# Decays of two more opening units by transfers, masks and exponentials; two more units turned on VectorE; a new order of work in an mLSTM + MLP kernel

## The chip, the cores and the metric

One core of one Trainium2 chip runs the whole program. The metric is the device time of one execution in microseconds (us); the kernel before stands at the median of three runs. Engines are named as in the profile: PE (TensorE's matmuls), PEld (its weight loads), DVE (VectorE), ACT (ScalarE), POOL (GpSimd), SP (SyncE, which here only issues transfers).

## The reference

An mLSTM layer (batch 4, 8 heads, 768 steps, head size 40) and behind it a feed-forward layer, all in float32:

```python
for t in range(S):
    m_new = np.maximum(f_gate[:, :, t] + m, i_gate[:, :, t])
    f_stab = np.exp(f_gate[:, :, t] + m - m_new)
    i_stab = np.exp(i_gate[:, :, t] - m_new)
    m = m_new
    C = f_stab[..., None, None] * C + i_stab[..., None, None] * np.einsum('bhd,bhe->bhde', vt, kt)
    n = f_stab[..., None] * n + i_stab[..., None] * kt
    y[:, :, t] = sigmoid(o_gate[:, :, t]) * (C @ qt) / max(|n @ qt|, 1)
x = y as [3072 tokens, 320]
h = x @ w_in                       # 320 -> 2048
out = (h * sigmoid(h)) @ w_out     # 2048 -> 320
```

## The kernel before

**Units.** The sequence is cut into 6 chunks of 128 steps. A unit is one chunk of one batch row with all 8 heads: unit n is chunk n // 4 of row n % 4, 24 in all. Units 0 to 3 are thus the first chunk. For a unit the kernel needs the decay matrix D, exp of a difference of running gate sums with the later keys masked out, in blocks of 64 steps. There are two ways to D:

- units below `WIDE` = 4 build it in PSUM on PE: `spread` (8 matmuls), `spans` (16) and `keys` (4) add up the exponent with its mask, and one ACT instruction takes the exponential of the whole tile (`exps_all`, L585);
- the others fetch the gate sums LF, which DVE computed and SP stored to DRAM (`LFd`), spread over partitions (`load_d`, two transfers, L500), set the masked half to -1e30 on POOL (`mask`, twice, L601), and take exponentials head by head on ACT (`exps`, two halves of four instructions, L595) with the key's term as bias. That term is `aT`, which `flip` makes on PE (L267, L272) and DVE copies out.

Then follow, for every unit: `column` (DVE, L615: values weighted by the last column of D), `products` (PE, L642: the state's increment), `carry` (ACT, POOL and DVE: the state), `scores` (PE, L679: q times k), `weigh` (DVE, L698: scores times D), `values` (PE, L716), `queries` (PE, L739: q scaled on POOL by L628, times the state) and `gate` (DVE, L757 to L770: division, output gate).

**Turning.** A unit's result x has tokens on partitions, and the feed-forward product wants features there. Units below `TURN` = 8 turn it with transposes on PE into PSUM (`xpose`, L798 to L801). The others turn 32x32 blocks on DVE (`turn`, L779), write them to DRAM in four transfers, and read them back as whole rows (`turned`). In both ways ACT then rounds the high part (L808) and DVE takes the low part (L812).

**The feed-forward part.** Every product is made of rounded high and low parts. The opening takes units 0 to 3 together (words with A, B, J), then ten steps take two units each. A block of the first product (L825) is 16 matmuls of 256 columns, one of the second (L1001) 12 of 320 columns; they are called dense here, the matmuls of units small. While the opening runs, the weights arrive and are unpacked from 64-bit numbers on ACT and DVE (L336 to L393).

**The order.** Nothing is scheduled by a tool: `ORDER` is a text of about 1,100 words, and `perform` runs through it and issues what each word names, so each engine's queue, SP's and POOL's too, is the order of the words. `m1.3` is the first product of step 1, block 3, `a b f F n` are its tanh, gating, high part, low part and second product; `d5 k5.0 e5.1 v5 P5 S5 w5 V5 Q5 g5 x5 i5 h5 y5` are unit 5's load, mask, exponentials, column, products, scores, weigh, values, queries, gate, turn, read back, high and low part; `s sp sb` are `spread`, `spans`, `keys`; `gs gu gm gt gf go` work on the gates of a chunk (`gf` is `flip`, `go` the store to DRAM), and `z7*2` issues two dummy matmuls of 512 columns (`spin`, L1025).

Of the kernel before, what the change touches and what calls it, by code (L numbers as in the profile page):

```python
# [56 lines left out]
h2 y2 Q3 bA3 mA2 aA1 g3 Mi3 Jo1 nA0 x3 Mi2 h3 Si2 aA2 k4.0 bA1 Si3 nA3 y3 mB0 bA2 aB0 nA1 Zi3 Lo3 mB3 Ji3 nA2 bB0 Ti3
Ri3 Mo2 aB3 Zi2 k4.1 bB3 mJ7 Ji2 gm2 Mo6 aJ7 nB0 So2 Li6 So6 mB2 Lc4 bJ7 Ti2 aB2 Ri2 Zo6 nB3 mJ4 Mo3 aJ4 Li4 e4.1 bB2
mJ5 So3 lq4 qk4 Jo6 go2 Lo4 d5 Mc4 aJ5 Zo3 lq5 bJ4 nB2 Li5 Jo3 mB1 nJ7 Zo2 Li7 Sc4 Mi4 Si4 Jo2 bJ5 l4 Zi4 e4.0 gt2 v4
mJ6 Ji4 Zc4 nJ5 Jc4 Mi6 d6 Si6 Ti4 S4.0 aB1 aJ6 Zi6 Tc4 bB1 k5.1 Ri4 Mo4 t4 qk5 P4 bJ6 kvo5 Rc4 So4 S4.1 Ji6 nJ4 Ti6 mJ8  # L60
mJ9 q4 w4 gf2 aJ8 Mi7 V4 kvo6 bJ8 Ri6 k6.0 k6.1 Zo4 Si7 e6.1 c4 d7 k5.0 Mi5 l5 Lo5 nJ6 aJ9 nB1 Si5 d8 bJ9 Jo4 Zi5 mJ13
e5.1 S5.0 Q4 mJ12 qk6 nJ8 e5.0 Ji5 Zi7 v5 aJ12 P5 aJ13 Ti5 bJ12 bJ13 S5.1 gl Ri5 Ji7 k7.1 w5 Mo5 mJ10 e6.0 mJ11 Ti7 So5
lq7 lq6 g4 t5 nJ9 Lo7 c5 k8.1 aJ10 v6 Zo5 bJ10 uh6 kvo7 fJ12 S6.0 k8.0 l6 Ri7 Jo5 aJ11 P6 k7.0 V5 S6.1 FJ12 mJ14 d10
nJ10 w6 fJ13 q5 Mo7 bJ11 Q5 ul6 FJ13 e7.0 So7 g5 x4 e7.1 mJ15 h4 uh0 nJ11 nJ13 y4 aJ14 e8.0 gs3 v7 lq8 nJ12 x5 Zo7 bJ14
aJ15 h5 fJ14 c6 qk7 bJ15 Jo7 y5 kvo9 P7 uh7 t6 V6 gu3 ul0 uh1 FJ14 e8.1 k10.0 m1.3 ul7 d9 m1.0 fJ15 k10.1 ul1 qk8 l7 q6
q7 kvo8 FJ15 Q6 l8 a1.3 b1.3 f1.3 nJ14 qk9 g6 F1.3 lq9 nJ15 a1.0 m1.1 v8 O2 t7 b1.0 O0 O1 S7 uh3 f1.0 t9 S8 m1.5 c7 w7
a1.1 t8 uh4 b1.1 F1.0 P8 w8 k9.1 ul3 a1.5 b1.5 V7 uh2 O3 l9 f1.1 m1.6 D2 q8 Q7 gm3 k9.0 ul2 lq11 F1.1 g7 uh5 e9.0 a1.6
c8 e9.1 n1.0 kvo10 n1.3 f1.5 F1.5 n1.1 m1.4 x6 D1 a1.4 v9 lq10 x7 e10.1 kvo11 h6 e10.0 b1.6 b1.4 ul4 P9 V8 ul5 f1.4 h7
d11 m1.2 qk11 y7 f1.6 m1.7 go3 F1.6 t10 n1.5 v10 y6 F1.4 a1.2 n1.4 b1.2 gt3 qk10 a1.7 l10 Q8 q9 b1.7 k11.0 D0 S9 qk12
f1.2 n1.6 F1.2 f1.7 m2.0 w9 F1.7 c9 gf3 a2.0 P10 lq12 V9 k11.1 l11 d12 q10 b2.0 S11 m2.4 e11.1 m2.2 a2.4 f2.0 t11 g8 S10  # L70
Q9 F2.0 qk13 b2.4 a2.2 n1.2 g9 f2.4 e11.0 m2.3 n1.7 O4 c10 x8 b2.2 v11 F2.4 w11 w10 m2.5 P11 O5 q11 kvo12 f2.2 V10 k12.0
F2.2 n2.0 a2.5 b2.5 n2.4 kvo14 lq13 a2.3 l12 n2.2 d13 i8 x9 S13 V11 d14 b2.3 h8 m2.1 c11 k12.1 k14.1 y8 D4 m2.6 i9 k13.1
f2.5 l13 F2.5 Q11 f2.3 F2.3 S12 Q10 lq14 n2.5 qk14 t12 a2.6 k13.0 a2.1 b2.1 e12.1 k14.0 h9 b2.6 d15 g10 D5 lq15 y9 f2.6
x10 e13.0 k15.1 e12.0 F2.6 v12 m2.7 f2.1 w12 F2.1 n2.3 m3.0 n2.6 q12 a2.7 b2.7 f2.7 m3.3 P12 i10 V12 e13.1 n2.1 F2.7
a3.0 kvo13 qk15 c12 b3.0 n2.7 a3.3 f3.0 g11 b3.3 q13 v13 m3.5 F3.0 O6 f3.3 t13 m3.1 w13 h10 Q12 a3.1 e14.1 d16 F3.3 S14
S15 P13 l14 O7 x11 b3.1 a3.5 V13 c13 n3.0 t14 n3.3 b3.5 l15 y10 g12 m3.2 f3.1 k15.0 f3.5 q14 kvo15 e14.0 d17 F3.1 F3.5
n3.1 D3 v14 k16.0 a3.2 b3.2 w14 Q13 i11 m3.4 e15.0 f3.2 kvo16 q15 F3.2 a3.4 n3.5 m3.7 h11 P14 qk17 lq16 b3.4 f3.4 x12
y11 qk16 i12 k17.1 V14 lq17 c14 m3.6 e15.1 F3.4 a3.7 b3.7 n3.4 D6 g13 f3.7 k16.1 a3.6 b3.6 n3.2 x13 m4.0 f3.6 k17.0 F3.6
Q14 m4.1 e16.0 F3.7 a4.0 l16 n3.6 d18 a4.1 v15 b4.0 b4.1 f4.0 n3.7 g14 F4.0 m4.2 t15 f4.1 kvo17 m4.5 D7 a4.2 w15 P15 O8
O9 e17.1 F4.1 kvo18 h12 a4.5 b4.2 S16 k18.1 b4.5 e16.1 v16 f4.2 V15 y12 e17.0 v17 m4.3 d19 F4.2 lq18 a4.3 c15 n4.0 f4.5  # L80
F4.5 m4.4 a4.4 n4.1 b4.3 D9 n4.2 qk18 f4.3 F4.3 m4.6 t18 n4.5 w16 x14 S18 b4.4 Q15 f4.4 k18.0 i13 l17 h13 F4.4 g15 lq19
a4.6 n4.4 m4.7 k19.1 y13 e18.0 q16 b4.6 q17 P16 f4.6 S17 V16 m5.0 a4.7 b4.7 F4.6 n4.3 n4.6 qk20 a5.0 f4.7 i14 m5.1 D8
e18.1 h14 F4.7 a5.1 c16 b5.0 n4.7 w17 f5.0 b5.1 k19.0 v18 Q16 x15 e19.0 O10 qk19 m5.2 m5.3 F5.0 a5.2 P17 f5.1 y14 l18
b5.2 V17 F5.1 O11 t16 c17 f5.2 kvo19 a5.3 i15 b5.3 m5.4 F5.2 d23 k23.1 w18 n5.0 a5.4 f5.3 g16 n5.1 F5.3 b5.4 h15 m5.6
D10 y15 f5.4 m5.5 n5.3 a5.5 b5.5 q18 F5.4 e19.1 Q17 a5.6 S19 S20 t19 P18 t17 V18 v19 d20 n5.2 n5.4 l19 b5.6 lq20 kvo20
# [1071 lines left out]
```

## Time and profile before

| what | value |
|---|---|
| median of 3 runs | 459.15 us (457.53 to 460.43) |
| the profiled execution, its own time | 458.83 us |
| its span, first to last instruction | 457.1 us |
| around the span | 1.73 us |
| PE / DVE / ACT / POOL busy in the span | 447.0 / 278.7 / 210.8 / 88.7 us |

Busy times count overlapping instructions once. The ends of matmuls are modelled by the profiler, so the length of a burst on PE is best read from its start to the start of the next one.

### The profile page before, as it was taken

The page shows a single profiled execution, that of the slowest core. Times are in us where ns is not written, and L with a number is a line of the kernel's source. Part 1 is how long each engine was busy: PE and PEld are TensorE (multiplying, and loading weights), DVE is VectorE, ACT ScalarE, POOL GpSimd, SP SyncE. Part 2 cuts the span into 40 slices and gives each one's busy share as a digit, 9 for nine tenths or more (in the row PEclk, how much of TensorE's full clock was granted, in tenths as well). Part 3 has the DMA queues.
Part 4 walks back from the last instruction along what each step waited for, and adds up shares of the span by engine and source line. Part 5 has one row for each costly group of instructions (what it writes and reads, how often), then busy time and mean ns, then how long its engine had stood idle before and what let it go on. Part 6 is the DMA issues. An engine that isn't in the chain of part 4 may idle for free.

```text
span 457.1 us, 13742 instructions
## 1 busy us (share of the span) xinstructions
PE 447.0 (98%) x5784; PEld 418.6 (92%) x5784; DVE 278.7 (61%) x559; ACT 210.8 (46%) x489; POOL 88.7 (19%) x125
## 2 busy tenths in 40 slices
...
GB/s 221 208 234 227 272 184 138 222 74 85 128 148 106 63 148 145 128 89 202 121 149 57 89 116 33 118 62 134 163 53 66 48 17 22 44 37 47 29 1 29
DMA packets 57293, 50.92 MB, mean 111 GB/s; under 512 B 29136, under 2 KB 47632, under 8 KB 57232
## 3 DMA queue, kind: packets, MB, share of 16 engines
...
q8 instruction: 45, 0.74, 0.7%
...
## 4 chain that ended last, share of the span: by engine, by line
PE 95%; DMA 2%; DVE 1%; issue 0%; ACT 0%; POOL 0%; SPq 0%; DVEq 0%; ACTq 0%; POOLq 0%
PE psum L825 41%; PE psum L1001 31%; PE psum L905 4%; PE psum L739 3%; PE psum L679 3%; PE psum L642 3%; PE psum L716 3%; PE psum L921 1%; PE psum L907 1%; DMA lq<-LFd 1%; PE psum L798 1%; PE psum L801 1%; DMA G<-in_ig_dram 1%; PE psum L908 1%; DMA LFd<-G 1%; PE psum L267 0%
## 5 line engine op out<-in xcount | busy, mean ns | idle before, releaser
L1001 PE MATMUL psum<-woh,g 128*128 128x320 f32 x640 | 150.7, 311 | 0.0
L1001 PEld LDWEIGHTS psum<-woh,g 128*128 128x128 f32 x640 | 109.1, 188 | 0.8
L1001 PE MATMUL psum<-wol,g 128*128 128x320 f32 x320 | 98.7, 308 | 0.0
L974 DVE SCALAR_TENSOR_TENSOR th<-th,psum 128x512 f32<-128x512 f32 x80 | 54.3, 682 | 69.4 <-ACT th L970 67.6
L970 ACT ACTIVATE th<-psum 128x512 f32<-128x512 f32 x80 | 47.4, 597 | 100.7 <-PE psum L825 86.5
L825 PE MATMUL psum<-xh,wh 128*128 128x256 f32 x480 | 84.7, 285 | 0.0
L825 PE MATMUL psum<-xl,wh 128*128 128x256 f32 x480 | 82.7, 280 | 0.0
L985 DVE TENSOR_TENSOR g<-th,g 128x512 fp32r<-128x512 f32 x80 | 57.6, 725 | 22.7 <-ACT g L981 21.7
L825 PEld LDWEIGHTS psum<-xh,wh 128*128 128x128 f32 x480 | 68.9, 188 | 1.0
L981 ACT CAST g<-th 128x512 fp32r<-128x512 f32 x80 | 49.2, 617 | 41.6 <-DVE th L974 27.4
L825 PEld LDWEIGHTS psum<-xl,wh 128*128 128x128 f32 x480 | 67.9, 188 | 0.0
L825 PE MATMUL psum<-xh,wl 128*128 128x256 f32 x320 | 63.8, 281 | 0.0
L1001 PEld LDWEIGHTS psum<-wol,g 128*128 128x128 f32 x320 | 60.1, 188 | 0.0
L825 PEld LDWEIGHTS psum<-xh,wl 128*128 128x128 f32 x320 | 49.1, 189 | 0.0
L601 POOL TENSOR_SCALAR_AFFINE_SELECT D<-D 64x512 f32<-64x512 f32 x40 | 29.4, 739 | 83.8 <-DMA D<-LFd 79.7
L628 POOL TENSOR_TENSOR qt<-raw,eq 104x512 f32<-104x512 f32 x24 | 34.3, 1428 | 43.3 <-PE psum L739 32.4
L595 ACT ACTIVATE D<-D,aT 128x64 f32<-128x64 f32 x160 | 41.8, 339 | 0.7 <-POOL D L601 0.7
L663 POOL TENSOR_TENSOR S<-S,eq 104x164 f32<-104x164 f32 x20 | 9.3, 464 | 137.5 <-DVE S L661 112.3
L825 PE MATMUL psum<-X,wh 128*128 128x512 f32 (+1 forms) x120 | 32.7, 389 | 0.0
L825 PEld LDWEIGHTS psum<-X,wh 128*128 128x128 f32 x120 | 21.5, 202 | 4.4 <-DVE g0J L892 0.2
L642 PEld LDWEIGHTS psum<-vw,kvo 64*64 64x64 f32 x704 | 15.0, 149 | 7.0 <-DVE vw L615 2.8
L642 PE MATMUL psum<-vw,kvo 64*64 64x41 f32 x704 | 17.8, 243 | 2.3 <-DVE vw L615 2.0
...
## 6 DMA issues: line engine op xcount, KB each, us to landing
...
```

What stands on the lines that cost most here:

```text
L595: nc.scalar.activation(d[:, j, :], e[:, j, :], AF.Exp, bias=aT[:, self.c, hf, r : r + 1])
L601: nc.gpsimd.affine_select(out=d, in_=d, compare_op=ALU.is_ge, fill=NEG, base=0, pattern=[[0, H], [1, LB]], channel_multiplier=-1,)
L628: nc.gpsimd.tensor_tensor(out=self.qt, in0=self.q[:KP], in1=self.eq, op=ALU.mult)
L642: m = nc.tensor.matmul(PU[hf * 64 : (hf + 1) * 64, k, j, :], self.kt[rs, h * D : h * D + 64], self.vw[rs, h, :], start=True, stop=True,)
L679: m = nc.tensor.matmul(self.ps[r * 64 : (r + 1) * 64, hf, j, :], self.k[rows, r ^ hf, j, :], self.q[rows, r ^ hf, j, :], start=True, stop= ...
L825: nc.tensor.matmul(ph, w, x, start=(i == 0), stop=(i == len(ops) - 1))
L905: nc.tensor.matmul(self.po[u][:, :DM], gs, w, start=(fc == 0), stop=False)
L970: nc.scalar.activation(th, self.ph[s], AF.Tanh, scale=0.5)
L974: nc.vector.scalar_tensor_tensor(out=th, in0=th, scalar=1.0, in1=ph, op0=ALU.add, op1=ALU.mult)
L981: nc.scalar.copy(t[:, 0], self.th[s])
L985: nc.vector.tensor_tensor(out=gl, in0=self.th.pop(s), in1=gh.bitcast(F32), op=ALU.subtract)
L1001: nc.tensor.matmul(self.po[t], g[:, ts], w, start=(fc == 0 and i == 0), stop=(last and i == 2),)
```

## The change

Units 2 and 3 (the third and fourth) no longer build their decays on PE: the limit in `exps` is now `EARLY` = 2, so they take the way by transfers, masks and head-by-head exponentials. `TURN` falls from 8 to 6, so units 6 and 7 are turned on DVE and through DRAM. The table is a new one from its first word to block 6.5, and the same again behind it but for the place of one word (`S22`). From it are gone `s2 s3 sp2 sp3 sb2 sb3`; new are `d2 d3`, four masks (`k2.0` to `k3.1`), `e2.0 e2.1 e3.0 e3.1` for `e2 e3`, `gf0` (the key's terms of the first chunk) and `i6 i7`; `z7*2` has become `z7*4`.

```diff
 WIDE = 4
+EARLY = 2
...
-TURN = 8
+TURN = 6
...
 ORDER = """
-gs0 Li1 Li0 s1 gu0 s0 gm0 kvo0 gt0 gs1 go0 sp0 sb0 gu1 Mi1 qk0 Mi0 e0 Si1 lq0 sp1 Si0 s2 t0 l0 Zi1 v0 kvo1 sp2 Zi0 lq1
+gs0 s0 gs1 Li0 gs2 Li1 Lc0 gu0 gm0 gt0 kvo0 go0 qk0 lq0 kvo1 gu2 Mi0 gf0 sb0 sp0 s1 Mi1 sp1 S0 sb1 gu1 e0 Mc0 Si0 Si1
...
         def exps(self, hf=None):
-            if self.n < WIDE:
+            if self.n < EARLY:
                 return self.exps_all()
             d = e = self.Dm[:, hf * HF : (hf + 1) * HF, :]
```

On PE, in the opening, the kernel before issues from unit 2's `spans` (L561) to the beginning of unit 3's `spread` (L536):

```order
L561 MATMUL psum<-G,ident 64x64 x16
L642 MATMUL psum<-vw_244,kvo_174 64x41 x16
L679 MATMUL psum<-raw_139 64x64 x16
L574 MATMUL psum<-minus,G 64x256 x8
L642 MATMUL psum<-vw_320,kvo_246 64x41 x16
L716 MATMUL psum<-kvo_174,D_209 64x41 x16
L679 MATMUL psum<-raw_140 64x64 x16
L536 LDWEIGHTS one
L536 MATMUL psum<-past,one 64x256
```

The changed kernel issues in that place on PE (its lines stand two further on; L563 is `spans` of unit 1, L269 and L274 are `flip` of the third chunk):

```order
L563 MATMUL psum<-G,ident 64x64 x16
L681 MATMUL psum<-raw_139 64x64 x16
L576 MATMUL psum<-minus,G 64x256 x4
L644 MATMUL psum<-vw_275,kvo_172 64x41 x16
L718 MATMUL psum<-kvo_172,D_260 64x41 x16
L681 MATMUL psum<-raw_140 64x64 x16
L741 MATMUL psum<-S_1_128,qt_310 64x41 x8
L269 MATMUL psum<-ident,G 128x16
L274 MATMUL psum<-ident,G 64x16 x2
L644 MATMUL psum<-vw_352,kvo_182 64x41 x16
```

The bursts of units 2 and 3 are gone from between those of units 0 and 1, unit 0's `queries` (L741) have moved ahead of unit 1's `products` (the last row), and a `flip` stands between.

On SP, the queue of transfers, the kernel before begins with these after the gates:

```order
L321 DMA wri_149<-in_w_in_dram 128x2x512
L321 DMA wri_151<-in_w_in_dram 128x2x512
L489 DMA kvo_174<-in_kvo_dram 128x968
L283 DMA LFd<-G 16x2x64 x2
L480 DMA raw_139<-in_qk_dram 40x1024 x2
L512 DMA lq_142<-LFd 40x2x256 x2
L489 DMA kvo_246<-in_kvo_dram 128x968
L512 DMA lq_143<-LFd 40x2x256 x2
L480 DMA raw_140<-in_qk_dram 40x1024 x2
L489 DMA kvo_304<-in_kvo_dram 128x968
```

The changed kernel's SP begins with these (`wrc` are weights, `LFd` the stored gate sums, `lq` and `D` what is fetched of them, `raw` q and k, `kvo` k, v and the output gate):

```order
L323 DMA wri_158<-in_w_in_dram 128x2x512
L323 DMA wri_161<-in_w_in_dram 128x2x512
L326 DMA wrc_163<-in_w_in_dram 64x2x512 x2
L491 DMA kvo_172<-in_kvo_dram 128x968
L285 DMA LFd<-G 16x2x64 x2
L482 DMA raw_139<-in_qk_dram 40x1024 x2
L514 DMA lq_142<-LFd 40x2x256 x2
L491 DMA kvo_182<-in_kvo_dram 128x968
L514 DMA lq_143<-LFd 40x2x256 x2
L482 DMA raw_140<-in_qk_dram 40x1024 x2
L502 DMA D_305<-LFd 64x2x256 x2
L514 DMA lq_142<-LFd 40x2x256 x2
```

Two weight transfers have moved ahead of unit 0's `kvo` and the store of the gate sums, and unit 2's decay is fetched behind unit 1's q and k, ahead of unit 2's `lq`.

On PE, in step 1, the kernel before turns units 6 and 7 between two blocks of the first product, next to unit 9's `products`:

```order
L825 MATMUL psum<-xl_1424,wh 128x256 x3
L798 MATMUL psum<-ident,x_1648 128x128 x3
L798 MATMUL psum<-ident,x_1865 128x128 x3
L642 MATMUL psum<-vw_1948,kvo_1497 64x41 x16
L716 MATMUL psum<-kvo_1599,D_1113 64x41 x16
```

In the changed kernel PE has no such rows for these units; in that place it goes from a block of step 1 to unit 9's `products` and the `flip` of the late gates:

```order
L827 MATMUL psum<-xl_1381,wh 128x256 x3
L644 MATMUL psum<-vw_1907,kvo_1501 64x41 x16
L269 MATMUL psum<-ident,lfi 128x16
L274 MATMUL psum<-ident,lfi 64x16 x2
```

The six transposes of units 6 and 7 have left PE; two instructions of L781 on DVE, eight writes and two reads on SP stand for them.

## Rows read from the trace of the kernel before

**Rows 1.** The page: busy time by engine; the chain that ended last; ACT's exponentials.

```profile
PE 447.0 (98%) x5784; PEld 418.6 (92%) x5784; DVE 278.7 (61%) x559; ACT 210.8 (46%) x489; POOL 88.7 (19%) x125
...
PE 95%; DMA 2%; DVE 1%; issue 0%; ACT 0%; POOL 0%; SPq 0%; DVEq 0%; ACTq 0%; POOLq 0%
...
L595 ACT ACTIVATE D<-D,aT 128x64 f32<-128x64 f32 x160 | 41.8, 339 | 0.7 <-POOL D L601 0.7
```

**Rows 2.** Windows: length, busy time by engine (instructions), granted clock, DMA share, GB/s.

```profile
3.46:32.14 28.68, 24.78 (x529) 18.62 (x525) 22.81 (x53) 11.61 (x23) 7.95 (x11) 1.00 0.74 222
5.49:34.90 29.41, 26.84 (x595) 21.08 (x595) 23.09 (x50) 12.09 (x24) 6.04 (x7) 1.00 0.75 227
34.90:113.58 78.68, 78.68 (x786) 64.39 (x785) 64.37 (x123) 41.39 (x99) 19.13 (x23) 1.00 0.57 170
113.58:309.95 196.37, 196.17 (x2929) 190.91 (x2927) 119.13 (x248) 96.40 (x237) 47.76 (x62) 1.00 0.40 111
```

**Rows 3.** Timeline of PE, opening: start us, length us, what, [idle before <-releaser].

```profile
15.50 1.09 PE L642 MATMUL psum<-vw,kvo 64*64 64x41 f32 x32 [1.99 <-DVE vw L615]
...
18.30 0.64 PE L536 MATMUL psum<-past,one 32*64 32x256 bf16 x8
18.73 1.07 PE L561 MATMUL psum<-G,ident 16*64 16x64 f32 x32
19.73 1.08 PE L739 MATMUL psum<-S,qt 40*64 40x41 f32 x16
20.74 1.13 PE L574 MATMUL psum<-minus,G 16*64 16x256 f32 x8
...
23.14 0.60 PE L267 MATMUL psum<-ident,G 16*128 16x16 f32 x2
23.67 0.40 PE L272 MATMUL psum<-ident,G 16*64 16x16 f32 x4
23.99 1.08 PE L739 MATMUL psum<-S,qt 40*64 40x41 f32 x16
...
30.00 1.01 PE L1025 MATMUL psum<-G 128*128 128x512 bf16 x2
...
34.90 1.00 PE L825 MATMUL psum<-X,wh 128*128 128x256 f32 x3
```

**Rows 4.** Chain that ended last: start us, length us, what.

```profile
8.53 3.80 DMA lq<-LFd
...
34.97 3.71 PE psum L825 x16
...
123.39 2.10 PE psum L825 x16
...
136.63 0.66 PE psum L798 x6
...
159.03 1.96 PE psum L1001 x12
...
162.88 1.76 PE psum L1001 x12
164.64 1.87 PE psum L825 x16
...
446.74 7.05 PE psum L1001 x48
```

**Rows 5.** By line: instruction, ns min/median/max, first and last start, forms.

```profile
L615 DVE TENSOR_TENSOR vw<-kvo,D x4: 489/494/1305, 8.3 to 30.7; 128x328 f32<-128x328 f32 x4
...
L601 POOL TENSOR_SCALAR_AFFINE_SELECT D<-D x40: 648/657/1410, 44.0 to 318.5; 64x512 f32<-64x512 f32 x40
...
L779 DVE STREAM_TRANSPOSE y<-x x16: 566/572/578, 162.0 to 407.1; 128x384 f32<-128x384 f32 x16
```

**Rows 6.** Timeline of POOL, opening.

```profile
13.82 1.27 POOL L628 TENSOR_TENSOR qt<-raw,eq 104x512 f32<-104x512 f32 x1
...
43.96 1.28 POOL L601 TENSOR_SCALAR_AFFINE_SELECT D<-D 64x512 f32<-64x512 f32 x1 [5.61 <-DMA D<-LFd]
```

More of the change, by code (lines that the diff above doesn't have):

```diff
@@ L57 @@
[L57 to L85, printed above, removed]
-c18 f5.5 k20.1 F5.5 m5.7 f5.6 d21 m6.0 F5.6 a5.7 n5.5 b5.7 a6.0 f5.7 b6.0 m6.4 F5.7 lq21 n5.6 k20.0 f6.0 g17 n5.7 F6.0
```

67 lines of the change are left out of this document (49 added, 18 removed).

## The prediction

> **What bounds the kernel now.** I read first the page's busy times and the chain that ended last: PE is busy 447.0 of 457.1 us, and 95% of the chain lies on it [rows 1]. Then the windows, to see where PE is not full. From 34.90 us, where the first dense block starts, to 113.58 it is busy without a gap, and to 309.95 it idles 0.20 us; only the opening has room, with 26.84 busy of 29.41 us between the first `spans` at 5.49 and the first dense block [rows 2]. So the end is one sum: the time of the first dense block, plus the length of everything PE issues behind it, plus whatever gaps the new order opens. Last I read PE's timeline in the opening and the dense blocks in the chain. Sixteen matmuls of 256 columns take 3.71 us at 34.97 and 1.87 us at 164.64 [rows 4]: PE runs at 1.2 GHz in the opening and at 2.4 GHz later, though the windows print a granted clock of 1.00 for both [rows 2]. Up to the first dense block, therefore, small bursts cost about 1 us each.
>
> **The opening.** Two units lose three bursts each on PE: `spread` 18.30 to 18.73, 0.43 us; `spans` 18.73 to 19.73, 1.00; `keys` 1.13 [rows 3]. That is 2.56 us, twice 5.1. Unit 3's `products` move behind the first dense blocks (about 0.9, the length of such a burst by its row at 15.50 less the overlap). Added are one more `flip`, 23.14 to 23.99, 0.85 us, and two dummy matmuls, 1.01 [rows 3]. PE has 4.1 us less to do before the first dense block.
>
> It can't take all of it, for DVE stands close behind. DVE was busy 22.81 of the 28.68 us that end with the low part of unit 1's x at 32.14 [rows 2], and the first dense block needs that part. In the new order the same word has more ahead of it on DVE: the third chunk's scans, differences and sums, one more copy of `aT`, more unpacking of weights. Adding up the lengths of that queue by line, from the rows of before, gives 26.9 us against 24.8 (with overlaps counted), 2.1 more. If DVE idles as before (5.87 us), unit 1's low part comes at 34.2, and the dense block with it: 0.7 us earlier than 34.90. The bounds: 30.8, if PE alone decides (34.90 less 4.1), and 37.4, if DVE idles as before and each of the four new masks also stretches a DVE instruction as far as the one long `column` was stretched, 1305 against 494 ns, four times 0.81 [rows 5]. I take 34.2, which stands on a busy row of DVE.
>
> What covers the rest: unit 2 and 3 now need eight exponentials each, 16 times 0.339 [rows 1] for two instructions of about 0.6; ACT was busy 11.61 of 28.68 us [rows 2], so its 4.2 us more find room. Four masks at 0.66 to 1.41 us [rows 5] go to a POOL that was busy 7.95 [rows 2]; behind them on POOL wait the scaled queries of units 1 and 2, and behind those Q1, the `gate` of unit 1 and its x. If that cover goes, a mask's length is added to the opening.
>
> **At the place of the masks** the trace shows one collision: of four `column` instructions three took 0.49 us and one 1.305 [rows 5], and while it ran POOL scaled the queries of unit 0 from 13.82 on for 1.27 us [rows 6]; PE then waited 1.99 us for that `column` [rows 3]. The Trainium skill says why, in "SBUF — State Buffer", section "Who interferes with whom": VectorE with two SBUF inputs and GpSimd reading SBUF take turns on one port, and the later one "fully blocks". That bears on this change, for a mask reads SBUF and most of DVE's opening work has two inputs there; by the rule every mask costs its length on one of the two engines, and the sum would be 458.0, the lost opening among the rivals below. The row agrees with it once, and three of four `column` instructions were not touched.
>
> **From the first dense block on.** I cut PE's timeline into its bursts, from the one at 34.90 [rows 3] to the last blocks at 446.74 [rows 4], 293 words of the order, and took the median length of each kind by its neighbours. A dense block costs 0.1 us more for each side that touches small bursts: second products 1.76 between dense ones and 1.96 beside a small one at the far end of this spread, first products 1.87 and 2.10 with small ones on both sides [rows 4]. Put together, the old order gives 414.7 us to the start of the last block; measured are 417.0, and the 2.3 between are the first blocks at the slow clock. The new order gives 411.4, 3.2 less: 0.75 for the six transposes (their row shows 0.66 plus a switch [rows 4]), 1.1 for eleven fewer sides of dense blocks that touch small bursts (66 before, 55 now), 1.0 in the opening's second products for the same reason, 0.8 in `values` and `queries` that now stand in company, and 0.44 back for unit 3's `products`. DVE takes two turns more, 0.57 each [rows 5], of which 13 us of idle time in 34.90 to 113.58 [rows 2] and more later are the cover; the eight writes and two reads go to a queue whose share there is 0.57 and 0.40.
>
> A new order can also open gaps on PE. Adding up DVE's words against PE's, the second product of block 0 of the pair (word `nB0`) is left 0.8 us of room, where the old order left 3.7; the next narrow place has 3.6. I allow 0.5 us.
>
> **Sum.** Minus 0.7, minus 3.2, plus 0.5 is minus 3.4 on the profiled execution's 458.83: 455.4 us. That execution lies 0.32 under the median of 459.15, so it is 0.8% under the median. About 1% of it, 4.6 us (454.6 or 463.7), is what a measurement here can tell from no change.
>
> **The clock** stays an unknown on both sides. Before, the rate doubled after the first two dense blocks had run slowly [rows 4]. If the two added dummy matmuls bring that forward to before the dense blocks, the 2.3 us of slow blocks go, and about 1 in the three small bursts between; if one more pair of blocks runs slowly, 1.9 us are added (3.71 less 1.87). I take it as before.
>
> **Rivals.** *PE sets the opening.* DVE's idle time shrinks instead of staying, and the dense block starts at 30.8: minus 4.1 and 3.2 gives 451.5. For it: 5.87 us of DVE's idle time were waits for PE, transfers and other engines, several of which the new order asks for earlier. Against: its queue is 2.1 us longer. *The opening is lost.* DVE and POOL hold each other up, by four masks' shortest length, 2.6 us, on the path to unit 1's x: 458.0, no change. For it the `column` of 1305 ns, against it the other three. *Transfers set the opening* (slower). The store of the gate sums now stands on SP behind two more weight transfers, and all of units 0 to 3 waits for what is fetched of it; unit 0's fetch took 3.80 us [rows 4] in a stretch that already moves 222 GB/s [rows 2], and a later unit's D was waited for 5.61 us by POOL [rows 6]. From unit 2's `products` on, PE has seven bursts before the first dense block in the new order, about 8.6 us at the lengths that these bursts have on the old timeline (the four dummies, 2.0, among them [rows 3]), so they must begin by 25.6. Each us later is a us on the end; from 29.0 on the kernel is slower than before, and at 34 it ends at 463.8. Against: unit 2's D is asked for right behind unit 1's q and k, some 12 us before it is needed.
>
> **Chances.** Forecast 0.45, its own range 453.5 to 457.3 (0.09 of it beyond 1%); PE sets the opening 0.29 (0.27 beyond 1%); opening lost 0.12; transfers 0.14 (0.08 beyond 1% slower). Faster by over 1%: 0.36; within 1%: 0.56; slower: 0.08. The range reaches from 450.5, a little below the first rival (its time with half of the clock's gain), to 460.5, which leaves out most of the fourth.
>
> **What will show it.** Right: the first dense block starts at 33.5 to 35, PE has under 1 us of gaps behind it, and from there to the end it takes about 413.7 us to its last block. The opening step is wrong if the dense block starts before 32.5 or after 36; then the row before the gap says whether DVE, POOL or a transfer was late. The dense step is wrong if PE idles more than 1 us behind 35, or if blocks beside small bursts don't cost 0.1 us more. A doubling of the rate before the dense blocks would make the clock wrong.

## The result, and the profile after

The changed kernel takes 462.86 us (median of 17 runs, 460.60 to 467.47) against 459.66 (17 runs, 456.99 to 461.40): the ratio is 1.0088, with a 95% interval from 1.0063 to 1.0113. It is 0.9% slower; 455.4 was forecast, and the median lies above the range's end of 460.5. The profiled execution took 463.50 us and its span is 461.3.

The page of the changed kernel, the same two lines as in [rows 1]:

```profile
PE 443.3 (96%) x5689; PEld 415.6 (90%) x5690; DVE 285.5 (62%) x562; ACT 214.3 (46%) x503; POOL 93.3 (20%) x129
...
PE 83%; DVE 5%; DMA 4%; issue 4%; ACT 2%; POOL 1%; SPq 0%; DVEq 0%; POOLq 0%; ACTq 0%
```

PE is busy 3.7 us less, where the sum had 4.1 less ahead of the first dense block and 3.2 less behind it, and the span is 4.2 us longer: the chain that was 95% PE is now 83%, and 16% of it are other engines, transfers and time that the profile calls issue. The windows say where. The first two answer to the second and third of [rows 2]; then come step 1 and 2, a piece of it, and what follows:

```profile
6.63:36.82 30.19, 24.13 (x481) 18.94 (x482) 22.75 (x50) 14.12 (x36) 11.83 (x11) 1.00 0.78 239
36.82:114.20 77.38, 77.17 (x821) 62.99 (x817) 65.64 (x129) 43.39 (x103) 21.27 (x26) 1.00 0.62 183
114.20:205.00 90.80, 87.85 (x1343) 84.62 (x1342) 59.05 (x113) 45.51 (x116) 20.94 (x29) 0.98 0.42 114
141.40:144.90 3.50, 3.50 (x17) 3.50 (x16) 2.92 (x7) 0.00 (x0) 1.07 (x2) 0.51 0.51 155
205.00:314.00 109.00, 109.00 (x1578) 106.59 (x1577) 64.08 (x126) 50.75 (x123) 22.12 (x28) 1.00 0.39 105
```

Three things are new. The first dense block starts at 36.82 and not at 34.90. Between 114.20 and 205.00 PE idles 2.95 us (90.80 less 87.85), where it had 0.20 in twice that stretch. And from 141.40 to 144.90 the granted clock is 0.51, half rate, with PE busy all the time. Behind 205 nothing is lost. The last block starts at 456.16, before at 451.85: of the 4.3 us, 1.9 arise before the first dense block and 2.4 behind it.

**The opening.** PE's timeline from 6 us on, the rows with a wait over 0.6 us, and the first dense block (for the old ones see [rows 3]):

```profile
6.63 0.61 PE L269 MATMUL psum<-ident,G 16*128 16x16 f32 x2 [2.89 <-DVE G L258]
11.70 0.44 PE L681 MATMUL psum<-raw 40*64 40x64 f32 x2 [1.07 <-DMA raw<-in_qk_dram]
...
18.19 1.71 PE L681 MATMUL psum<-raw 40*64 40x64 f32 x32 [1.75 <-DMA raw<-in_qk_dram]
...
24.21 1.02 PE L681 MATMUL psum<-raw 40*64 40x64 f32 x27 [0.64 <-DMA raw<-in_qk_dram]
...
30.95 0.69 PE L800 MATMUL psum<-ident,x 128*128 128x128 f32 x2 [0.83 <-DVE x L772]
...
36.82 0.62 PE L827 MATMUL psum<-X,wh 128*128 128x256 f32 x3
```

The scores of units 0, 1 and 2 wait for q and k, which they did not do before. Up to the first dense block PE has 2.7 us less to do (24.13 in place of 26.84), but its first burst comes 1.1 later (6.63 in place of 5.49) and it waits 6.1 us in place of 2.6: together 1.9 later. The waits for q and k in these rows are 3.5 us of that. The last wait is another: unit 1's x comes late from DVE, which had stood 0.73 us for output weights that ACT unpacks, and ACT 3.40 us for their transfer:

```profile
28.83 0.49 DVE L346 TENSOR_SCALAR wto<-wto 128x640 uint32<-128x640 uint32 x1 [0.73 <-ACT wto L338]
```

```profile
28.02 0.78 ACT L338 ACTIVATE wto<-wro 128x640 f32<-128x640 f32 x1 [3.40 <-DMA wro<-in_w_out_dram]
```

From there PE runs to the dense block with no wait over 0.23 us. The last row of PE has a second message: its three matmuls take 0.62 us, and those at 34.90 took 1.00 [rows 3], so PE already ran at 2.4 GHz at its first dense block. Why q and k are late stands on SP, first the changed kernel's queue:

```profile
6.28 0.82 SPq L285 DMA_DIRECT2D LFd<-G  x2
7.23 0.69 SPq L482 DMA_DIRECT2D raw<-in_qk_dram  x2
10.96 0.68 SPq L514 DMA_DIRECT2D lq<-LFd  x2
...
12.91 1.56 SPq L482 DMA_DIRECT2D raw<-in_qk_dram  x2
```

and the same rows of the kernel before:

```profile
5.46 0.82 SPq L283 DMA_DIRECT2D LFd<-G  x2
6.33 0.75 SPq L480 DMA_DIRECT2D raw<-in_qk_dram  x2
8.14 0.69 SPq L512 DMA_DIRECT2D lq<-LFd  x2
...
11.09 0.71 SPq L480 DMA_DIRECT2D raw<-in_qk_dram  x2
```

The fetch `lq` may start only when the stored gate sums have landed. That store is issued 0.8 us later and behind two more weight transfers, and SP stands still from 7.92 to 10.96 (3.0 us; before, 7.08 to 8.14), so unit 1's q and k behind it are asked for 1.8 us later. The 0.8 us, and PE's late first burst with them, come from the order of DVE's words: `gs1 gs2` now stand ahead of `gu0`, so three scans run before the first gate sums where one did. First the changed kernel, then the one before:

```profile
3.52 1.44 DVE L223 TENSOR_TENSOR_SCAN G<-G 48x128 f32<-48x128 f32 x3 [2.61 <-DMA G<-in_ig_dram]
```

```profile
3.46 0.42 DVE L221 TENSOR_TENSOR_SCAN G<-G 48x128 f32<-48x128 f32 x1 [2.56 <-DMA G<-in_ig_dram]
```

These rows are one execution. The same opening in the traces of e2, e6 and e10 below starts its first dense block at 36.68, 37.85 and 37.54.

**Steps 1 and 2.** PE's rows with its pauses, in the changed kernel:

```profile
156.96 0.68 PE L644 MATMUL psum<-vw,kvo 64*64 64x41 f32 x32 [0.77 <-DVE x L766]
...
161.71 0.56 PE L1003 MATMUL psum<-woh,g 128*128 128x320 f32 x2 [0.79 <-DVE g L987]
...
203.42 0.56 PE L1003 MATMUL psum<-woh,g 128*128 128x320 f32 x2 [0.78 <-DVE g L987]
```

Each waits for DVE. DVE's timeline around the first and the last of them:

```profile
155.78 0.17 DVE L759 TENSOR_SCALAR nq<-psum 128x8 f32<-128x8 f32 x1 [5.36 <-PE psum L741]
...
200.23 1.02 DVE L772 SCALAR_TENSOR_TENSOR x<-kvo,x 128x320 f32<-128x320 f32 x1
201.29 1.16 DVE L776 COPY x<-x 128x64 f32<-128x64 f32 x1
202.36 1.00 DVE L987 TENSOR_TENSOR g<-th,g 128x512 fp32r<-128x512 f32 x1
```

At 155.78 DVE had stood 5.36 us at unit 8's `gate` (`g8`), because that needs `Q9`, which PE issues only behind block `m2.0`; the gatings that PE wants next queued behind it. At 200.23 it is another thing: three instructions run at 2.1, 5.9 and 1.5 times their usual 0.49, 0.195 and 0.69 us.

### The profile page after: what moved, and what is told of

The parts are those of the page before. It is cut to its first block, busy times and chain, and to the rows that moved or that the text cites. A ratio compares the mean times of both kernels' runs of the same rounds, so it can differ in the third digit from the quotient of the medians.

```text
span 461.3 us, 13611 instructions
## 1 busy us (share of the span) xinstructions
PE 443.3 (96%) x5689; PEld 415.6 (90%) x5690; DVE 285.5 (62%) x562; ACT 214.3 (46%) x503; POOL 93.3 (20%) x129
## 4 chain that ended last, share of the span: by engine, by line
PE 83%; DVE 5%; DMA 4%; issue 4%; ACT 2%; POOL 1%; SPq 0%; DVEq 0%; POOLq 0%; ACTq 0%
PE psum L827 36%; PE psum L1003 28%; PE psum L907 4%; DMA raw<-in_qk_dram 3%; PE psum L681 3%; PE psum L644 3%; PE psum L718 2%; PE psum L741 2%; PE psum L923 1%; ACT D L597 1%; PE psum L909 1%; DVE g L987 1%; POOL D L603 1%; DMA G<-in_ig_dram 1%; DVE th L976 1%
## 5 line engine op out<-in xcount | busy, mean ns | idle before, releaser
L597 ACT ACTIVATE D<-D,aT 128x64 f32<-128x64 f32 x176 | 46.0, 337 | 4.0 <-POOL D L603 4.0
L630 POOL TENSOR_TENSOR qt<-raw,eq 104x512 f32<-104x512 f32 x24 | 32.1, 1339 | 65.2 <-ACT eq L626 16.1
L603 POOL TENSOR_SCALAR_AFFINE_SELECT D<-D 64x512 f32<-64x512 f32 x44 | 35.2, 803 | 48.3 <-DMA D<-LFd 40.8
L665 POOL TENSOR_TENSOR S<-S,eq 104x164 f32<-104x164 f32 x20 | 10.7, 536 | 130.2 <-DVE S L663 124.7
L827 PE MATMUL psum<-X,wh 128*128 128x512 f32 (+1 forms) x120 | 29.9, 367 | 0.0
L681 PE MATMUL psum<-raw 40*64 40x64 f32 x768 | 21.2, 237 | 4.1 <-DMA raw<-in_qk_dram 3.7
L827 PEld LDWEIGHTS psum<-X,wh 128*128 128x128 f32 x120 | 20.1, 188 | 4.2 <-DVE den L761 0.2
L681 PEld LDWEIGHTS psum<-raw 40*64 40x64 f32 x768 | 17.5, 147 | 6.8 <-issue 5.0
```

The costliest lines, as they stand in the source:

```text
L597: nc.scalar.activation(d[:, j, :], e[:, j, :], AF.Exp, bias=aT[:, self.c, hf, r : r + 1])
L603: nc.gpsimd.affine_select(out=d, in_=d, compare_op=ALU.is_ge, fill=NEG, base=0, pattern=[[0, H], [1, LB]], channel_multiplier=-1,)
L630: nc.gpsimd.tensor_tensor(out=self.qt, in0=self.q[:KP], in1=self.eq, op=ALU.mult)
L681: m = nc.tensor.matmul(self.ps[r * 64 : (r + 1) * 64, hf, j, :], self.k[rows, r ^ hf, j, :], self.q[rows, r ^ hf, j, :], start=True, stop= ...
L827: nc.tensor.matmul(ph, w, x, start=(i == 0), stop=(i == len(ops) - 1))
```

## The experiments

Theories. **Transfers:** the opening is late because the decays of units 2 and 3 put 512 KB more into a queue whose share is already 0.75. **Clock:** dense blocks at half or full rate move the time by 2 us either way, and small bursts decide it. **Order:** a few words stand on DVE in front of what PE needs. **All from the opening** (rival): the late start pushes the rest out of step. **Turning** (rival): the round trip through DRAM costs more than the six transposes. Each kernel is compared with the kernel before on the same chip; "clock fell" counts runs with a mean granted clock of 0.996 or less. Of the 17 runs of the changed kernel 10 had that (median 463.6), 7 not (462.4).

**Opening against rest, crossed (e1, e2).** e1 has the old words up to the first dense block:

```diff
-EARLY = 2
+EARLY = 4
-gs0 s0 gs1 Li0 gs2 Li1 Lc0 ... v3 l3 S3 Q2 w3 mA0 aA0 mA3
+gs0 Li1 Li0 s1 gu0 s0 gm0 ... V2 S3 w3 Q2 mA0 aA0 mA3
```

> The old kernel's words up to the first dense block (units 2 and 3 built on PE again, two dummies), then the new kernel's words in their order (units 6 and 7 still turned on VectorE). Theory 'two places' (the opening loses 2.0 us at the first dense block and gets 2.3 back from the earlier clock; the loss that shows at the end lies in the stretch 115 to 205 us): first dense block at 34.9 us, full rate only behind two dense blocks, the half-rate dip near 141 us and the pauses near 155 to 163 and 202 us still there, so 461 to 464 us, no better than the changed kernel. Rival 'all from the opening' (the late start pushes everything behind it out of step): the pauses go and the new order's 3.2 us come in: 455 to 457 us.

e2 has the new words up to there and the old ones behind:

```diff
-TURN = 6
+TURN = 8
-mA0 aA0 mA3 g2 bA0 t3 gf1 P3 V3 ...
+mA0 mA3 g2 gf1 P3 x2 c3 q3 Lo2 V3 ...
```

> The mirror image: the new kernel's words up to the first dense block (units 2 and 3 by transfers and masks, four dummies), then the old kernel's words (units 6 and 7 turned on PE again). 'Two places': first dense block at 36.8 us, full rate from about 35.6 us, no dip near 141 us, no pauses behind 115 us: 458.5 to 460.5 us, the same as before. 'All from the opening': 462 to 464 us, as slow as the changed kernel.

Measured: e1 464.29 (ratio 1.0114, 1.0083 to 1.0146), e2 464.37 (1.0121, 1.0094 to 1.0148). e1's first dense block starts at 35.19 and the kernel is no faster: "all from the opening" falls, and the pauses at S11, n1.4 and n3.0 are all there. But "two places" had e2 at 458.5 to 460.5, and that is wrong too. Its window:

```profile
36.68:118.68 82.00, 80.43 (x820) 65.66 (x817) 64.22 (x121) 41.20 (x101) 18.27 (x23) 0.96 0.55 161
42.80:49.60 6.80, 6.21 (x35) 5.52 (x36) 5.50 (x14) 0.93 (x2) 1.92 (x3) 0.50 0.75 205
```

After an early rise the clock fell again for 6.80 us; all six runs have a mean granted clock of 0.996 or less. PE had only small bursts and waits from 38.8 to 43.4 (V3 took 2.38 us in place of 0.58, 1.40 of them waits). Each half is about 5 us slower by itself; what the two have in common is that the clock or a wait takes back what the sum gives.

**The dummies alone (e3).**

```diff
-z7*2
+z7*4
```

> The kernel before with four dummy matmuls in the place of two, nothing else. If the dummies are what made the clock rise before the dense blocks: first two dense blocks at 1.9 us in place of 3.7, first dense block at 35 to 36 us: 457 to 458.5 us, faster by 1 to 2.3. Rival (the clock rose in the changed kernel because small bursts, flip and dummies together stood closer, and not by the dummies): the two added dummies, 1.0 us, only lie on the path: 459.5 to 460.5.

Measured 456.42, ratio 0.9947 (0.9927 to 0.9967): 2.8 us faster, the best kernel of the study, and faster than both. Its first dense block:

```profile
33.89 0.62 PE L825 MATMUL psum<-X,wh 128*128 128x256 f32 x3
```

0.62 us where the kernel before took 1.00: the rise came before it. That the block starts 1.0 us earlier though two dummies were added is more than the clock explains: unit 1's scores started 1.3 us earlier in this execution.

**The transfers alone (e9), and the early decays alone (e7).** e9 leaves every instruction of the kernel before and adds the loads, into a part of X that is written later:

```diff
-... Zi1 v0 kvo1 sp2 Zi0 lq1 P0 qk1 ...
+... Zi1 v0 kvo1 sp2 Zi0 lq1 d2 d3 P0 qk1 ...
```

> The kernel before, whole, with the four transfers of the decays of units 2 and 3 (512 KB in rows of 1 KB) added behind unit 1's gate sums, where the kernel with the early decays alone had them; what they fetch is not used (it goes to memory that is overwritten before it is read). Theory 'the bytes in the queue': unit 1's q and k land 1.5 to 2 us later, its scores start near 18 us in place of 17.2, and with all of PE's bursts still there the first dense block starts at 36 to 37.5 us: 460 to 462 us. Rival 'masks, exponentials and VectorE' (the loads lie beside other work): first dense block within 0.4 us of 34.9 and 458.5 to 459.7 us.

Measured 461.58, 1.0056 (1.0038 to 1.0074). Rows of its PE:

```profile
18.27 0.44 PE L682 MATMUL psum<-raw 40*64 40x64 f32 x2 [0.42 <-DMA raw<-in_qk_dram]
...
37.69 1.01 PE L828 MATMUL psum<-X,wh 128*128 128x256 f32 x3
```

Four transfers that nobody uses move the first dense block from 34.90 to 37.69: 2.8 us, and the ratio says 2.6. But they stand ahead of unit 1's q and k on SP, and the issuing alone takes SP 2.61 us there:

```profile
10.91 2.61 SPq L503 DMA_DIRECT2D X<-LFd  x4
13.63 1.10 SPq L480 DMA_DIRECT2D raw<-in_qk_dram  x2
```

So q and k are asked for 2.5 us later than before (11.09), and this run does not part the bytes of the loads from their place. In the changed kernel the loads stand behind unit 1's q and k. e7 has the early decays whole, in the old order:

```diff
+EARLY = 2
-gs0 Li1 Li0 s1 gu0 s0 gm0 kvo0 gt0 gs1 go0 sp0 sb0 gu1 ... lq1 P0 ... q0 e2 gm1
+gs0 Li1 Li0 s1 gu0 s0 gm0 kvo0 gt0 gs1 go0 sp0 sb0 gf0 gu1 ... lq1 d2 d3 P0 ... q0 k2.0 k2.1 gm1
```

> The kernel before with only units 2 and 3 taken over to transfers, masks and exponentials (old order otherwise; decays asked for behind unit 1's gate sums, two dummies). 'Transfers and masks take the place of the 5.1 us': first dense block not before 34.5 us and the time 458.5 to 462, no gain. Forecast's own rival 'PE sets the opening': first dense block at 31 to 32.5 and 455 to 457.

Measured 460.76, 1.0034 (1.0009 to 1.0059), first dense block at 36.36. So with the loads in both, taking away PE's six bursts (5.1 us), with a `flip`, masks and exponentials added, moves the first dense block by 37.69 less 36.36, 1.3 us. That is one execution of each; by the ratios it is 1.0 us, and their intervals overlap. In e7's opening PE waits for DVE at five places, 1.33, 1.55, 1.25, 0.89 and 1.29 us, where e9 has 1.33, 2.40, 0.25 and 0.84, and 1.53 us for q and k, where e9 has 0.88. That is 2.1 us more in all: a good part of what is taken off PE goes into waits.

**The place in the queue (e4, e5).** Two attempts to mend the opening by moving transfers; both missed.

```diff
-... t1 w1 k2.1 Tc0 Lo0 gt2 Q0 Li3 k2.0 l1 g0 d3 e2.1 ...
+... t1 w1 k2.1 Tc0 d3 Lo0 gt2 Q0 Li3 k2.0 l1 g0 e2.1 ...
```

> The changed kernel with unit 3's decay asked for ahead of the 640 KB of output weights, nothing else. If transfers set the opening: the decay lands 3 us or more earlier than 30.7 us, unit 3's masks run before DVE's last work of the opening, exponentials e3 no longer hold up the high part of x1 on ACT, and the first dense block starts at 34.5 to 36 us in place of 36.8: 460 to 462 us, 1 to 2 below the changed kernel. If VectorE's longer queue or the mask's port sets it: first dense block within 0.5 us of 36.8 and no change of time.

Measured 464.01 (1.0105, 1.0073 to 1.0137), no gain. Its profiled execution took 469.83, so only the order of events is read: unit 3's first mask ran at 27.77 and not at 30.71, but the second stayed behind unit 2's state on POOL (33.58), and PE in its last 6 us before the dense block waited for neither. The late mask was not what set it.

```diff
-... Li1 Lc0 gu0 ... e0 Mc0 Si0 Si1 Sc0 ... Zc0 ... Ri1 Jc0 ...
+... Li1 gu0 ... e0 Si0 Si1 ... qk1 Lc0 ... Ri1 Mc0 Sc0 Zc0 ... k2.1 Jc0 ...
```

> The changed kernel with the two transfers of the column weights (512 KB) asked for behind unit 1's q and k in place of ahead of unit 0's data, and their unpacking moved behind with them. If the queue of transfers sets the opening: q and k of units 0 and 1 land about 2 us earlier, unit 1's scores start at 15.5 to 17 us in place of 18.2, the first dense block at 34.5 to 35.5 in place of 36.8, and the time falls by 1.5 to 2.5 us to 460.5 to 461.5. If it is VectorE or the masks: the scores come earlier but the first dense block stays within 0.5 us of 36.8 and the time within 0.5 us of the changed kernel.

Measured 468.85 (1.0208, 1.0177 to 1.0239), 6 us worse than the changed kernel. ACT and PE of it:

```profile
21.16 0.66 ACT L338 ACTIVATE wtc<-wrc 128x512 f32<-128x512 f32 x1 [6.58 <-DMA wrc<-in_w_in_dram]
```

```profile
18.22 0.45 PE L681 MATMUL psum<-raw 40*64 40x64 f32 x2 [3.41 <-DMA raw<-in_qk_dram]
19.34 1.13 PE L681 MATMUL psum<-raw 40*64 40x64 f32 x30 [0.68 <-DMA raw<-in_qk_dram]
```

With the weights behind the store, SP's standstill is gone: `lq` is issued at 8.03 in place of 10.96. So the 3.0 us were the place of the two weight transfers. But unit 1's q and k, asked for at 9.97 in place of 12.91, came at the same time, 18.2, with the weights now issued 0.75 us behind them (10.72) and unit 2's decay behind those. That the transfers issued behind them held them up is likely, but not shown by itself. And the unpacking, moved with the weights, held ACT for 6.58 us, with unit 0's state behind it.

**The order of steps 1 and 2 (e6, e10).**

```diff
-... l11 lq13 m2.0 Q9 g8 S11 P10 ...
+... l11 lq13 Q9 g8 m2.0 S11 P10 ...
-... b3.2 g11 k15.1 m3.3 F3.0 v13 ...
+... b3.2 F3.0 g11 k15.1 m3.3 v13 ...
```

> The changed kernel with two places of its order mended, nothing else: unit 9's queries and gate (Q9 g8) ahead of the block m2.0, and the gating F3.0 ahead of unit 11's gate. Theory 'order on VectorE': the pauses of PE at S11 (0.95 us over the usual length), n1.4 (1.2) and n3.0 (1.05) go: 2 to 3 us less than the changed kernel, 460 to 461. Rival 'collisions with GpSimd': the stretched instructions (0.2 to 1.2 us, 0.49 to 1.6) only hit another consumer and the time stays within 0.7 us of the changed kernel's 462.9.

Measured 460.97, 1.0045 (1.0015 to 1.0075): 2.0 us less than the changed kernel by the ratios (0.43% of 459.66; the two intervals overlap), and S11, n1.4 and n3.0 have their usual lengths. The clock still fell in 9 of 12 runs (in its trace from 143.4 on, behind the same bursts). Its first dense block, at 37.85, ran at half rate (1.01 us for the first three matmuls): the early rise of the changed kernel's opening does not come in every execution. e10 moves one more word:

```diff
-... f1.6 P9 x7 gf3 b1.2 V9 S8 n1.1 h6 ...
+... f1.6 P9 x7 b1.2 V9 S8 n1.1 gf3 h6 ...
```

> The changed kernel with the two places on VectorE mended as before, and the flip of the late gates (gf3) moved from between unit 9's products and values to behind the block n1.1. Theory 'the pack of small bursts lets the clock fall': no half rate near 141 us in any run, every run's mean granted clock 0.999 or more, 458.5 to 460 us, 1 to 2 below the kernel with the two places alone. Rival (the dip is not due to the pack, or three small bursts do the same): the clock still falls in most runs, 460.5 to 461.5.

Measured 459.05, 1.0016 (0.9987 to 1.0044), and the clock fell in 1 of 12 runs. Its window of about the same words (m1.0 to m3.5):

```profile
115.71:203.50 87.79, 86.79 (x1346) 83.19 (x1345) 55.57 (x112) 47.07 (x122) 21.42 (x29) 1.00 0.45 118
```

PE idles 1.00 us where it idled 2.95, at full rate. Four words moved take 3.3 us off (1.0088 less 1.0016, of 459.66), and the changed kernel is level with the one before. In the changed kernel PE did P9, gf3, V9 and S8 without a dense block from 137.34 to 140.77, and then the rate fell; without gf3 in the pack it fell in only 1 of 12 runs.

**Turning (e8, e13, e16; e11 against e12).** e8 is the kernel before with units 6 and 7 turned on DVE:

```diff
-TURN = 8
+TURN = 6
-... m1.4 x6 D1 ... x7 e10.1 kvo11 h6 ... f1.4 h7 d11 ... y7 f1.6 ... v10 y6 F1.4 ...
+... m1.4 x6 i6 D1 ... x7 e10.1 kvo11 ... f1.4 h6 y6 d11 ... f1.6 ... v10 i7 F1.4 ... h7 y7 gt3 ...
```

> The kernel before with only units 6 and 7 turned on VectorE and through DRAM (their six transposes gone from PE, old order otherwise). By the sum: 0.75 us less, 458.4, at best. Rival: the small bursts now stand without cover and the rounding on ACT waits for the transfers (6.3 us in the changed kernel), and the rate falls for a while near 141 us: 459.5 to 461.

Measured 465.63, 1.0139 (1.0104 to 1.0174). DVE and PE of it:

```profile
139.94 0.58 DVE L779 STREAM_TRANSPOSE y<-x 128x384 f32<-128x384 f32 x1 [4.34 <-DMA xd<-y]
```

```profile
141.14 1.01 PE L825 MATMUL psum<-xh,wh 128*128 128x256 f32 x3 [3.08 <-DVE th L974]
```

The second turn waited 4.34 us for the first one's rows to leave, and PE 3.08 us behind it: that is the price of two turns close together, not of a turn. A part of the time is the clock's: it fell in 5 of 6 runs, in the trace twice, to 0.50 from 141.10 to 144.50, with this wait, and from 158.10 to 161.50. e13 puts the turns far apart, on e3:

```diff
-TURN = 8
+TURN = 6
-... g6 F1.3 ... S7 ... g7 ... x6 D1 ... x7 e10.1 kvo11 h6 e10.0 ... h7 ... y7 ... v10 y6 F1.4 ...
+... g6 x6 F1.3 ... S7 i6 ... g7 h6 y6 ... D1 ... x7 e10.1 kvo11 e10.0 i7 ... v10 h7 y7 F1.4 ...
```

> The kernel before with four dummies and units 6 and 7 turned on VectorE, the two turns 10 us apart (unit 6's right behind its gate, read back early). By the sum: 0.75 us less than with four dummies alone (456.4): 455.7 us, no wait of PE near 137 to 141 us. Rival 'a turn on VectorE costs more than three transposes anyway' (its writes and reads, ACT's wait for the rows): 457 to 459 us.

Measured 463.11, 1.0085 (1.0056 to 1.0114). Unit 7's turn ended at 134.48, ACT took its rows at 141.78 after a wait of 3.14 us, and DVE at 142.33, with the gating for n1.4 behind it; PE waited 2.35 us, and then the clock fell. e16 takes those rows later:

```diff
-... v10 h7 y7 F1.4 a1.2 n1.4 b1.2 gt3 ...
+... v10 F1.4 a1.2 n1.4 b1.2 h7 y7 gt3 ...
```

> As the run with the turns apart (old kernel, four dummies, units 6 and 7 turned on VectorE), but the high and low part of unit 7's turned rows taken only behind the next gatings, ahead of the third chunk's late gates. By the sum over bursts 0.75 us less than four dummies alone: 455.7 us, no pause of PE over 0.5 us between 120 and 150 us. Rival 'the round trip through DRAM (about 8 us from turn to rows in the last run) leaves no place free of waits here': 457 to 460 us.

Measured 458.22, 0.9988 (0.9968 to 1.0008). The six transposes are gained: from the first to the last dense block PE is busy 414.05 us, and 414.77 in e3, 0.72 less, where the sum had 0.75. But PE idles 1.96 us there, and 0.66 in e3. Two of its waits are 0.66 at 127.05, where unit 7's scaled queries are late and SP's queue had stood at the read of unit 6's turned rows (e13 has it too, e3 not), and 0.90 at 282.40 (0.26 in e3; not traced). So it is no better than e3's 0.9947: the gain is there and goes into waits, and 7.3 us from turn to rows (e13) make waits easy to create. The pair in the new order, both with the old opening, four dummies and the four moved words. e11 is e1 with these; e12 has the six transposes back:

> The old kernel's opening (units 2 and 3 on PE) with four dummies, then the changed kernel's words with the two places on VectorE and the flip mended, units 6 and 7 turned on VectorE. If the sum over PE's bursts was right and the loss lies only in the opening, the clock and those places: first dense block at 33.9 us and, from there, 3 us less than in the kernel before with four dummies: 453 to 454.5 us. Rival 'the order gives its gain back in other waits': 456 to 459 us.

```diff
-TURN = 6
+TURN = 8
+... w8 x6 h6 y6 ... c9 x7 h7 y7 ...
```

> The same with units 6 and 7 turned on PE again. By the sum the six transposes cost 0.75 us: 453.7 to 455.2 us, 0.5 to 1 above its twin. Rival 'turning through DRAM costs more than it saves here' (ACT waited 6.3 us for unit 7's turned rows): 0.5 to 2 us below its twin.

Measured: e11 458.31 (1.0000, 0.9983 to 1.0017), e12 460.62 (1.0043, 1.0019 to 1.0066). Here turning on DVE is worth 2 us. A part is the clock: it fell in 1 of 12 runs of e11 and 7 of 12 of e12, where the transposes stand right behind `gf3` (in its trace it falls at 142.4, with x6 and x7). It is not the whole, for the runs without a fall differ as well, 458.29 against 459.99 by their medians: in e12's trace PE waits 0.96 us for unit 8's `weigh` ahead of the transposes, and the transposes take their 0.75. Both miss their forecasts; e11 came where "the order gives its gain back in other waits" had it. In e11's trace, its one run with a fall (46.4 to 49.8), PE idles 2.75 us behind the first dense block, 0.79 and 1.17 of them for DVE at 39.91 and 44.80.

**What the order of the ten steps is worth (e14, e17).** The old words with four dummies up to block m1.3, the new ones with the moved words behind. In e14:

```diff
+... e8.1 k10.0 kvo8 d9 qk8 t8 t7 q6 l7 k9.0 Q6 fJ15 g6 FJ15 ul7 m1.3 m1.0 k9.1 x6 ...
```

> The old kernel's words with four dummies up to the first block of step 1, then the changed kernel's words with the two places on VectorE and the flip mended. If the new order loses its gain in the opening's blocks (second products in a row, waits of Q3, x3): block m1.0 at 111 us as with four dummies, and 2.5 us less from there: 454 to 455.2. Rival 'the ten steps give nothing either': 456 to 457.5.

Measured 464.41 (1.0108, 1.0074 to 1.0142), and the clock fell in 5 of 5 runs: PE waited 4.72 us at nJ14 for split weights whose word `ul7` stood behind `t8`, which waited for its data. e17 moves those:

```diff
-... kvo8 d9 qk8 t8 t7 q6 l7 k9.0 Q6 fJ15 g6 FJ15 ul7 m1.3 ...
+... q6 fJ15 FJ15 Q6 g6 ul7 kvo8 d9 qk8 l7 k9.0 m1.3 ... O2 t7 ... S7 t9 ... a1.1 t8 ...
```

> As the run with the old words up to step 1 and the new ones behind, with unit 7's and 8's output gates and the split weights put where their data has come, so that PE doesn't wait for them. If the new order of the ten steps is worth the 2.5 us of the sum over bursts: 454 to 455.2 us. Rival 'it gives them back in waits': 456 to 457.5 us, the same as four dummies alone.

Measured 458.39 (1.0002, 0.9976 to 1.0028); a wait of 1.7 us at the same place is left, and the clock fell behind it in the trace and in 4 of 12 runs, so the total decides nothing. The stretch behind it does: from block n1.0 to the last block e17 takes 321.82 us and e3 322.76, both at full rate, with 0.47 and 0.27 us idle. The new order of the steps gives 0.9 us in this pair of executions, where the expectation from the sum over bursts was 2.5; it is not waits that took the rest. Of the 0.9, 0.7 are the six transposes.

One more kernel is the changed one with `EARLY = 4` and its order kept. It does not compute the layer (where it goes astray was not traced), so its time decides nothing, but its transfers can be read.

```diff
-EARLY = 2
+EARLY = 4
-... d2 lq2 ... k2.1 ... k2.0 ... d3 e2.1 ... e2.0 ... k3.0 ... k3.1 ... e3.0 ... e3.1
+... s2 sp2 P0 ... S1 sb2 s3 sp3 ... Q0 sb3 ... e2 ... e3 ...
```

> The changed kernel with the decays of units 2 and 3 built on PE again, their loads, masks and the first flip gone, its order kept otherwise. 'Transfers alone': unit 1's q and k land 1 to 2 us earlier but PE has its six bursts (5.1 us) back: first dense block at 36 to 38 us, 461.5 to 464. Rival 'the new order of the queue is at fault too' (weights ahead of the store of the gate sums, which the fetches wait for): first dense block later than 38 us and 464 to 467.

Measured 465.71 (1.0147, 1.0113 to 1.0182), and the first dense block starts at 39.65, the mark of "the new order of the queue is at fault too" (later than 38). Without the 512 KB of the decays SP still stands idle behind the store, from 7.88 to 11.73 (`lq` is issued at 11.73), and unit 1's scores start at 19.56, later than the 18.19 of the changed kernel. PE waits 2.02 us there for unit 0's state on POOL, which came after ACT had waited 5.67 us for the fetched `lq`. So the order of the queue delays the opening without these bytes. How much of the 1.9 us is the order and how much the bytes no run here parts.

## Why the prediction was wrong

**The opening, −0.7 forecast, +1.9 measured. This step failed first.** What failed is its condition, "if DVE idles as before (5.87 us)". From 3.46 to the end of unit 1's low part at 36.87 DVE was busy 25.6 us, 0.7 more than the forecast's 24.9 (22.81 and 2.1), and idle 7.8 in place of 5.87. It stood because the engines ahead of it stood: PE for q and k, ACT for weights, and at the end ACT 2.85 us for unit 3's mask:

```profile
36.31 0.56 DVE L814 TENSOR_TENSOR X<-psum,X 128x384 fp32r<-128x384 f32 x1 [1.54 <-ACT X L810]
```

PE's own queue ran until 36.82 too, with waits of 0.22 and 0.23 us, so this last wait alone set nothing. The sum charged nothing for transfers: not for the new place of the store, behind two weight transfers and three scans, where SP stood 3.0 us in place of 1.1 (without the weights ahead of it the standstill is gone, e5), and not for the 512 KB that two decays fetch in a stretch that already moved 222 GB/s at a share of 0.74 [rows 2]. At that rate they are 2.4 us of the queue; e9 measured 2.8, its issuing included. How the 1.9 us divide between the two is open: in e15 unit 1's scores are late without the bytes, in e5 its q and k without the standstill. The 4.1 us that PE was to save were worth about 1 (e7 against e9), so the bound of 30.8 was never near. The rival "transfers set the opening" had the mechanism, the store behind two more weight transfers. It also had the size: unit 2's `products` began at 27.57, 8.6 us more is 36.2, and the first dense block came at 36.82. By its own mark (slower from 29.0 on) the opening alone would not have made the kernel slower. I gave it 0.14 on the ground that unit 2's D was asked for early; late were unit 0's, 1's and 2's q and k.

**The clock, "as before".** Wrong on both sides. It rose before the dense blocks, as the first alternative said, which is worth about the 2.3 us of slow blocks (e3: 2.8 us with the earlier start). The early rise does not come in every execution of this opening (e6). And the clock fell in 10 of 17 runs, in the trace near 141. The text had room for one more pair of slow blocks (1.9 us), but at the start and not in the steps: 1.2 us between the medians of the runs with and without, about 1.5 in the trace.

**The sum over PE's bursts, −3.2.** The lengths were right where the neighbours were those of the table: blocks beside small bursts cost 0.1 us more, as before. But five second products of the opening now stand directly before another one, and took 1.08 and 2.16 us where the same before a first product took 0.84 and 1.92: 5 times 0.24 is 1.2 us. The 1.0 us counted as gained in "the opening's second products" is thus lost, and for the steps 0.9 came where 2.5 was expected (e17). The 0.75 for six transposes did come as work (0.72, e16), and went into waits.

**Gaps, +0.5 allowed. This step failed by the most.** From the first dense block to the last PE took 419.3 us, where 413.7 was forecast, and the slow blocks had gone as well: 7.9 us more than the bursts' usual lengths. By place: 0.95 at S11, 1.20 at n1.4, 1.05 at n3.0, 0.47, 0.31 and 0.28 at Q10, Q11 and V10, 1.5 by the clock, 1.2 by the second products in a row, and 1.0 in pieces under 0.3. e6 and e10 took 3.3 of it away with four words. I had added up DVE's lengths against PE's, and so saw that DVE had room; I did not ask what each word on DVE waits for. `g8` behind `Q9` behind `m2.0` is such a wait, visible in the order alone.

**The masks.** The bound of 37.4, with every mask meeting DVE, was close to what came, but not because of the masks: e9 has none of them and came to 37.69, and moving the late mask gained nothing (e4). But the collisions are there, and more of them: a mask of 2.74 us where 0.66 is usual, and in steps 1 and 2 the stretched instructions above. One row each of the changed kernel and of the one before, all instructions of the copy that fills up a unit's result before it is turned:

```profile
L776 DVE COPY x<-x 128x64 f32<-128x64 f32 x18 | 7.4, 411 | 0.6
```

```profile
L774 DVE COPY x<-x 128x64 f32<-128x64 f32 x18 | 3.8, 211 | 0.6
```

The same 18 instructions take twice as long: 4 of them run while GpSimd masks or scales queries, at 1.16 to 1.17 us in place of 0.195; before, the longest took 0.34. All but the last 0.06 us of the one at 201.29 lie in this row:

```profile
199.61 2.78 POOL L630 TENSOR_TENSOR qt<-raw,eq 104x512 f32<-104x512 f32 x2
```

That is what the Trainium skill says in "SBUF — State Buffer", section "Who interferes with whom": VectorE's instructions with two inputs in SBUF, and copies in a mode that takes two ports, take turns with GpSimd's reads on one port. This trace agrees, and shows that what decides is whether PE waits for the one that is held up: n3.0 did.

Put together on the two traces: 1.9 in the opening, less 3.2 of the sum and 2.3 of slow blocks, plus 7.9, is 4.3.
